# A decode kernel that streams its K and V caches: four batches interleaved over the partitions in 16 KB runs instead of two in 8 KB runs, with a permuted transpose and a new path to P^T

## The chip, the cores and the metric

The kernel runs on one core of one Trainium2 chip. The metric is the device time of one execution in microseconds (us). Before the change the median was 224.2 us in the first three runs (223.59 to 224.71). A run counts as slow when it is over 1.5% above the fastest of the same kernel.

Words used below. SBUF is the on-chip memory of 128 *partitions*; PSUM is the accumulator memory that TensorE writes. SP is the engine that issues nearly all of this kernel's DMA transfers, in program order. A *slot* is one buffer of a ring: a transfer into it may only be issued when the last user of its old content is done. The *granted clock* is the share of full speed that the throttle gave TensorE.

## The reference, cut to what matters

```python
# B=4 batches, one token each, D=576; 32 query heads on 16 K/V heads of 128; last 2048 cached tokens; F=4608
xn = layernorm(x)
q  = (xn @ wq)                                    # wq: 576 x 4096
s  = q . k_cache[:, :, -2048:, :] * 128**-0.5     # 4 x 32 x 2048 scores
p  = softmax(s)
o  = p . v_cache[:, :, -2048:, :]
a  = o @ wo                                       # wo: 4096 x 576
h  = gelu(layernorm(xn) @ w1)                     # then shifted, @ w2, added to xn -> x1
h2 = gelu(layernorm(x1) @ w3) @ w4                # w3: 576 x 4608, w4: 4608 x 576
out = x + a + x1 + h2
```

K and V are 33.5 MB each; the weights bring the bytes that must be read to 88.5 MB. At the 420 GB/s that the profile shows below this is 211 us: the kernel is a stream of reads with some arithmetic that has to fit beside it.

## The kernel before: the parts that matter

K and V are read in 32 units of 1 MB each. A unit is one K/V head of two of the four batches: partition p = 2i + b holds 32 consecutive tokens of batch b, so each partition receives a run of 8 KB.

```python
NKU = 7            # K slots of 1 MB
NVU = 9            # V slots of 1 MB
...
def kv_pairs(ring_t, slot, cache, u):
    g, pr = u // 2, u % 2
    return [(ring_t[:, slot * UE:(slot + 1) * UE],
             cache[pr:B:2, g, Sk - W:Sk, :].rearrange("b (i t) d -> i b (t d)", t=NT))]     # NT = 32
for u in range(NU):                              # NU = 32: all of K first
    ev_k.append(add_dma(kv_pairs(kring_t, u % NKU, A_k_cache, u), ("k", u % NKU),
                        [f"T{4 * (u - NKU) + 3}"] if u >= NKU else [], u))
wo_wait = f"T{4 * last_unit(NKU, 0, (_o - 1) // UE) + 3}"      # wo, w1, w2 reuse the K slots
for u in range(NU):                              # then V0..V8, wo, V9, V10, w1, w2, V11...
    w = [f"PV{u - NVU}"] if u >= NVU else (["q"] if u < WQ_SLOTS else [])
    ev_v.append(add_dma(kv_pairs(vring_t, u % NVU, A_v_cache, u), ("v", u % NVU), w, kk))
    if u == WO_AFTER - 1:                        # WO_AFTER = 9
        ev_wo = add_dma(..., "wo", [wo_wait], kk + 0.005)
...                                              # w3, and w4 in pieces of 12, 12, 8, 3 and 1 row tiles
```

K arrives with tokens on the partitions. TensorE transposes each 128x128 block of it with the identity, DVE and ACT copy the results from PSUM, and the scores are matmuls over the transposed K. After the last score comes the softmax. P is needed transposed too, and each batch of a unit needs zeros where the other batch's tokens lie:

```python
ins = e.transpose(tb[n % NTB][:, t, :], kring[:, u % NKU, 8 * k + t, :], ident_bf[:])       # T<n>
...
for q in range(4):                     # exp of 64 rows at a time, written interleaved into a zeroed P_sb
    for bh in range(2):
        s = slice(64 * bh, 64 * bh + 64)
        e.activation(out=P_sb[s, 8 * q:8 * q + 8, :, bh], in_=Sps[s, q, :]..., func=ACTF.Exp, ...)
...                                    # P^T: 32 transposes 128x128, four copies of 128x1024 out of PSUM
```

The probabilities times V are matmuls `PV<u>`; V slot u is free when `PV<u>` is done. A `T<n>` is a group of eight transposes; a K slot is free when the last group of its unit is done.

## Time and profile before

| | before |
|---|---|
| median of the first call | 224.45 us (four runs, 223.59 to 224.72) |
| span of the profiled execution | 223.1 us |
| DMA | 9 tenths or more in slices 2 to 38 of 40 |
| last byte of K landed (slowest of 16 DMA engines) | 96.7 us |
| last score done | 107.1 us |
| P^T ready | 118.8 us |
| last byte of w4 landed | 218.0 us |
| last output matmul done | 220.9 us |

The landing times come from the trace's semaphore updates: a transfer is split over 16 DMA engines, and "the first" and "the slowest" engine below stand for the first and the last of its 16 landings. Packet times and sizes come from the trace's packet records.

The first thing to look at is the table of 40 equal slices of the span (5.6 us each). Rows are TensorE's busy tenths, its granted clock in tenths, the busy tenths of the DMA engines, and the GB/s moved:

```profile
PE   0459999999999999997267722665993435997596
PEclk9999999999999999999755555555587555665579
DMA  6999999999999999999999999999999999999950
GB/s 249 426 420 422 420 422 419 420 422 416 419 422 417 417 422 420 420 420 417 422 414 413 412 412 419 422 417 419 420 420 417 422 416 426 419 414 410 409 210 1
```

DMA has no dip from slice 2 to slice 38, although TensorE is nearly full for the first half. Whatever the compute engines do, the queue always has a transfer that may start. The chain of waits, followed back from the end (start, duration, what), looks different at first sight; it runs through TensorE until 107 us, then through the softmax, then through DMA:

```profile
107.09 2.30 DVE rmax L357
...
117.81 1.03 ACT PT L379
118.98 1.01 PE ps L402 x32
120.00 13.21 DMA vring<-in_A_v_cache_dram
...
179.78 29.80 DMA vring<-in_B_w_dram
209.62 11.28 PE ps L423 x72
```

It names what released each step, not what the time is bound by. In the stretch before 118.98 us DMA never waits for TensorE: seven K slots, nine V slots and wo hold the work it does meanwhile. The kernel is bound by bytes until the first pieces of w4 are there, and by 72 output matmuls at the end. The transposes (L321) are the costliest group of TensorE, and the exponentials (L363) of the softmax; columns are busy time, mean ns of one, and the idle time before them with what ended it:

```profile
L321 PE MATMUL ps<-ident_bf,kring 128*128 128x128 bf16 x1024 | 66.7, 220 | 0.6 <-ACT regB L327 0.5
L363 ACT ACTIVATE P_sb<-ps,negb 64x512 bf16<-64x512 f32 x8 | 6.6, 824 | 2.6 <-DVE negb L358 2.5
```

The 0.6 us of idle time before 1,024 transposes says that TensorE, not DMA, paces the K stage: 5.39 us per head in the chain, while DMA needs about 4.95 us for its 2 MB.

### The profile page before, as it was taken

The numbers are of one execution on the slowest core, as the hardware profiler recorded it, in microseconds if no ns is written. First come the engines' busy times: TensorE is split into PE (matmuls) and PEld (weight loads), VectorE is DVE, ScalarE is ACT, GpSimd is POOL, SyncE is SP. The second block draws the span as 40 slices with busy tenths as digits, with TensorE's granted clock in tenths as the row PEclk, the third lists the DMA queues.
The fourth block names the chain that finished last, engine by engine and source line by source line (L and its number), as shares of the span: only waits on it lengthen the run. The fifth ranks groups of instructions, "written<-read, shape, count | busy, mean of one in ns | idle before, by whom it ended". The sixth has DMA issues, their size and how long they took to land.

```text
span 223.1 us, 6242 instructions
## 1 busy us (share of the span) xinstructions
PE 163.6 (73%) x2933; PEld 124.6 (56%) x2934; DVE 70.3 (32%) x124; ACT 62.1 (28%) x76; POOL 7.8 (4%) x14
## 2 busy tenths in 40 slices
PE   0459999999999999997267722665993435997596
PEld 0456777777777777775047722454573434576363
DVE  4803556666666556664441000051000000000000
ACT  2002555555555555555594000000200000000000
POOL 8500000000000000000000000000000000000000
PEclk9999999999999999999755555555587555665579
DMA  6999999999999999999999999999999999999950
GB/s 249 426 420 422 420 422 419 420 422 416 419 422 417 417 422 420 420 420 417 422 414 413 412 412 419 422 417 419 420 420 417 422 416 426 419 414 410 409 210 1
DMA packets 13682, 88.91 MB, mean 399 GB/s; under 512 B 1356, under 2 KB 1752, under 8 KB 4440
## 3 DMA queue, kind: packets, MB, share of 16 engines
q1 hardware_dynamic: 13640, 88.50, 96.1%
q8 instruction: 23, 0.38, 0.7%
q10 hardware_dynamic: 16, 0.01, 0.0%
q14 instruction: 3, 0.02, 0.0%
HBM read 88.49 MB, written 0.00 MB: 397 GB/s over the span
## 4 chain that ended last, share of the span: by engine, by line
DMA 43%; PE 40%; ACT 12%; issue 1%; DVE 1%; SPq 1%
DMA vring<-in_A_v_cache_dram 25%; PE ps L321 23%; DMA vring<-in_B_w_dram 13%; ACT regB L327 8%; PE ps L337 8%; PE ps L423 6%; DMA vring<-in_A_wq_dram 5%; ACT P_sb L363 3%; PE ps L402 2%; PE ps L309 1%; DVE rmax L357 1%; SPq L159 1%; PE ps L372 0%; ACT PT L379 0%; PE ps L294 0%
## 5 line engine op out<-in xcount | busy, mean ns | idle before, releaser
L321 PE MATMUL ps<-ident_bf,kring 128*128 128x128 bf16 x1024 | 66.7, 220 | 0.6 <-ACT regB L327 0.5
L321 PEld LDWEIGHTS ps<-ident_bf,kring 128*128 128x128 bf16 x1024 | 57.9, 98 | 14.1 <-issue 7.8
L328 DVE COPY regB<-ps 128x1024 bf16<-128x1024 bf16 x80 | 52.3, 687 | 36.0 <-PE ps L321 34.3
L327 ACT ACTIVATE regB<-ps 128x1024 bf16<-128x1024 bf16 x48 | 47.5, 1021 | 48.2 <-PE ps L321 48.2
L402 PE MATMUL ps<-PT,vring 128*128 128x4 bf16 x1024 | 30.6, 166 | 29.5 <-DMA vring<-in_A_v_cache_dram 26.7
L402 PEld LDWEIGHTS ps<-PT,vring 128*128 128x128 bf16 x1024 | 28.9, 103 | 33.6 <-DMA vring<-in_A_v_cache_dram 28.5
L337 PE MATMUL ps<-regB,Qpad 128*32 128x512 bf16 x256 | 17.6, 392 | 4.5 <-ACT regB L327 4.5
L513 ACT ACTIVATE h2T_sb<-ps 128x144 bf16<-128x144 f32 x1 | 0.3, 290 | 49.7 <-PE ps L507 49.7
L423 PE MATMUL ps<-kring,ORT 128*4 128x288 bf16 x64 | 13.7, 398 | 0.3 <-DVE ORT L441 0.3
L423 PE MATMUL ps<-vring,h2T_sb 128*4 128x288 bf16 x72 | 11.3, 328 | 2.6 <-DMA vring<-in_B_w_dram 2.6
L437 DVE TENSOR_TENSOR OTn<-ps,rinvB 128x64 bf16<-128x64 f32 (+2 forms) x3 | 0.6, 202 | 39.6 <-PE ps L402 39.6
L337 PEld LDWEIGHTS ps<-regB,Qpad 128*32 128x32 bf16 x256 | 5.3, 94 | 11.1 <-ACT regB L327 5.9
L423 PEld LDWEIGHTS ps<-vring,h2T_sb 128*4 128x4 bf16 x72 | 6.8, 96 | 6.8 <-DMA vring<-in_B_w_dram 2.7
L259 ACT ACTIVATE sd<-mv 4x1 f32<-4x1 f32 x3 | 0.6, 202 | 35.3 <-DVE mv L257 35.3
L423 PEld LDWEIGHTS ps<-kring,ORT 128*4 128x4 bf16 x64 | 7.0, 113 | 5.9 <-DVE ORT L441 0.4
L372 PE MATMUL ps<-ident_bf,P_sb 128*128 128x128 bf16 x32 | 4.1, 309 | 6.6 <-ACT P_sb L363 6.6
L475 DVE TENSOR_TENSOR x_bf<-ps,xn_bf 4x288 bf16<-4x288 f32 x2 | 0.9, 446 | 23.8 <-PE ps L470 23.8
L528 DVE CAST out_sb<-ps 4x288 bf16<-4x288 f32 x1 | 0.4, 446 | 24.0 <-PE ps L423 24.0
L372 PEld LDWEIGHTS ps<-ident_bf,P_sb 128*128 128x128 bf16 x32 | 3.1, 140 | 7.9 <-ACT P_sb L363 7.9
L363 ACT ACTIVATE P_sb<-ps,negb 64x512 bf16<-64x512 f32 x8 | 6.6, 824 | 2.6 <-DVE negb L358 2.5
L273 PE MATMUL ps<-ident_bf,xn_bf 4*128 4x4 bf16 x8 | 0.5, 166 | 8.8 <-DVE ragsrc L266 8.4
L498 PE MATMUL ps<-x1nT,regB 128*128 128x4 bf16 x144 | 5.2, 172 | 1.5 <-DMA regB<-in_B_w_dram 1.5
(78 smaller groups left out, 68.6 us busy)
## 6 DMA issues: line engine op xcount, KB each, us to landing
kring<-in_A_k_cache_dram SPq DMA_DIRECT2D x32, 1024.0 KB, 12.6
vring<-in_A_v_cache_dram SPq DMA_DIRECT2D x32, 1024.0 KB, 21.6
kring<-in_A_wo_dram SPq DMA_DIRECT2D x1, 4608.0 KB, 26.0
regB<-in_B_w_dram SPq DMA_DIRECT2D x4, 1152.0 KB, 27.0
vring<-in_A_wq_dram SPq DMA_DIRECT2D x4, 1024.0 KB, 7.9
vring<-in_B_w_dram SPq DMA_DIRECT2D x2, 1728.0 KB, 30.7
kring<-in_B_w_dram SPq DMA_DIRECT2D x2, 576.0 KB, 13.5
vring<-in_B_w_dram SPq DMA_DIRECT2D x1, 1152.0 KB, 30.2
```

The source lines that it names most:

```text
L159: e.dma_start(o_, i_).then_inc(S[skey], 16)
L309: ins = e.matmul(ps[:, 4 + (w % NTB), :], lhsT=zeros_bf[:, 0:128], rhs=zeros_bf[:, :], start=True, stop=True)
L321: ins = e.transpose(tb[n % NTB][:, t, :], kring[:, u % NKU, 8 * k + t, :], ident_bf[:])
L327: return "act", lambda e: e.activation(out=ktbuf[:, n % NKT], in_=tb[n % NTB], func=ACTF.Copy)
L328: return "dve", lambda e: e.tensor_copy(out=ktbuf[:, n % NKT], in_=tb[n % NTB])
L337: ins = e.matmul(Sps[32 * b:32 * b + 32, c4, :].rearrange("p (t i) -> p t i", t=8), lhsT=Qpad[:, g, b, :], rhs=ktbuf[:, n % NKT, :, bh:128:2],
L357: add("dve", lambda e: e.tensor_reduce(out=rmax[:], in_=Sps, axis=AX.XY, op=ALU.max), waits=[f"SC{G - 1}"], sig="rmax", key=KS)
L363: add("act", lambda e, q=q, s=s, bh=bh: e.activation(out=P_sb[s, 8 * q:8 * q + 8, :, bh], in_=Sps[s, q, :].rearrange("p (t i) -> p t i", t ...
L372: ins = e.transpose(PTps[q][:, t, :], P_sb[:, 8 * q + t, :, :].rearrange("p i b -> p (i b)"), ident_bf[:])
L402: ins = e.matmul(o_, lhsT=vring[:, u % NVU, t, :], rhs=r_, start=(t == 0), stop=(t == NT - 1))
L423: return e.matmul(ACC[h], lhsT=lhsT, rhs=rhs, start=start, stop=stop)
L498: ins = e.matmul(H2Tps[:, n, :], lhsT=w3main[:, r, lo:hi:st], rhs=x1nT[:, r, :], start=(r == 0 and n == 0), stop=False, skip_group_check=True)
```

## The change

The intent is longer runs for DMA and less work for ACT. A unit is now a K/V head of all four batches, 2 MB: partition p = 4i + b holds 64 consecutive tokens of batch b, a run of 16 KB. Transposing K with a permutation matrix instead of the identity sorts the columns by batch, so that scores read contiguous columns and the exponentials can take 128 rows at once. P^T is then made by 32x32 transposes on DVE and, for each of the four batches, a matmul with a quarter of a second permutation matrix, which moves that batch's rows to partitions 4i + b and leaves zeros elsewhere.

Units twice as large mean fewer slots: 3 for K and 4 for V, where there were 7 and 9 half as large. The four early V units are issued between the last K units, and wo, which reuses K slots, waits for the last transpose of K. The diff, cut to its core:

```diff
-NKU = 7
-NVU = 9
+NKU = 3
+NVU = 4
+V_EARLY = 4
...
-    NT = 32
+    NT = 64
...
+        def kv_src(cache, g):
+            return cache[:, g, Sk - W:Sk, :].rearrange("b (i t) d -> i b (t d)", t=NT)
+        def issue_k(g, key):
+            w = [f"T{8 * (g - NKU) + 7}"] if g >= NKU else []
...
+        for g in range(G):
+            issue_k(g, g)
+        for g in range(V_EARLY):
+            issue_v(g, G - V_EARLY + g - 0.5)      # ... K11 V0 K12 V1 K13 V2 K14 V3 K15
+        wo_wait = f"T{8 * (G - 1) + 7}"            # the last transpose of the last K unit
+        ev_wo = add_dma(..., "wo", [wo_wait], KS)
...                                                 # w1, w2, then V4.. as PV0.. free their slots
-        W4P = [(0, 3, 0), (3, 6, 2), (6, 8, 4)]
+        for c in range(8):                         # w4 in eight pieces (and two small ones)
...
-                    ins = e.transpose(tb[n % NTB][:, t, :], kring[:, u % NKU, 8 * k + t, :], ident_bf[:])
+                    ins = e.transpose(tb[n % NTB][:, t, :], kring[:, g % NKU, 8 * k + t, :], perm_bf[:])
...
+            add("act", lambda e, q=q, cs=cs: e.activation(out=P_sb[:, cs], in_=Sps[:, q, :], func=ACTF.Exp, ...
+            add("dve", lambda e, cs=cs: e.transpose(PTc[:, cs], P_sb[:, cs]), waits=[f"exp{q}"], ...
+        for m in range(16):
+            add("pe", ... e.matmul(PTps[m % 4], lhsT=permT[32 * b:32 * b + 32, :],
+                                   rhs=PTc[32 * b:32 * b + 32, 512 * q:512 * q + 512], start=True, stop=True), ...
...                                                 # 16 copies of 128x512 out of PSUM, 9 on DVE, 7 on ACT
```

Two smaller things come with it: wq and w3 are each read in two large transfers instead of four.

## The prediction

> **What bounds the kernel now.** The DMA engines. The table of 40 slices shows DMA at 9 tenths or more from slice 2 to 37, 409-426 GB/s. In the trace's packet records an 8192-byte packet takes 312 ns, 4608 bytes 181 ns, 9216 bytes 351 ns; the slowest of the 16 engines lands the last of w4 at 218.0 us, the first at 212.8. The chain of waits runs through TensorE until 107 us, but DMA never pauses there: while TensorE finishes K (5.39 us per head in the chain) and the softmax runs (107.1 to 118.8 us), the queue still holds V units and wo. The tail is TensorE's: 72 output matmuls, 209.6 to 220.9 us, start when the first 1.7 MB of w4 lands and end 2.9 us after the last landing; the clock is 0.5 for their first 4.7 us.
>
> **What the change does.**
> 1. 16 KB runs. From 312 and 351 ns I estimate 618 ns per 16 KB packet instead of 624: about 290 such packets per engine, -1.8 us.
> 2. w4 in eight pieces instead of three: the matmuls can start at about 10 us before the last landing instead of 8.4, and end about 0.9 us after it instead of 2.9: -2.0 us.
> 3. Half as many exponentials (128 rows instead of 64; 0.82 us and a 0.18 us accumulator read each): about -3.5 us of ACT. But four DVE transposes and 16 evacuations of 128x512 f32 (estimate 0.6 us each, from 2.29 us for 2048 f32 and 1.02 us for ACT's 1024) replace four evacuations; they take some 8 us after the first exponential. Softmax from the last score to P^T ready: about 13 us, against 11.8 now.
> 4. Transposes and scores: as before, 5.39 us per head.
> 5. The order of transfers. Before, K is read first, and nine V units follow while TensorE catches up. Now four 2 MB V units go before the last K unit, and wo waits for the last K transpose. The Trainium skill ("DMA: Bandwidth & Descriptors", Anatomy of one DMA) says a semaphore wait sits on the issuing sequencer, not in the DMA engines; so SP stops there, with nothing queued behind K15, and DMA stands idle while TensorE transposes the last unit: 5.4 us warm. But TensorE will have idled 3-5 us between the last K units, which arrive every 9.9 us; "TensorE: Matmul & The Clock Gate" (Part 1) has the clock halve after an idle window of about 3.4 us, and here it fell 1.5 us after the scores ended. I take 7.5 us, plus about 1.5 us from issue to first byte: +9.0 us.
> 6. wo, w1, w2 (about 15 us) then cover the softmax and the first PV product (2 us): together about 16 us after the last transpose. V4 waits for that PV: +1 us (0 to 4).
> 7. Three K slots against 5.39 us per head and 4.94 us of DMA per unit: around units 7-11 DMA starts to wait for slots: +0.5 us.
>
> **On the critical path:** 1, 2, 5, 6, 7. Sum: 224.2 - 1.8 - 2.0 + 9.0 + 1.0 + 0.5 = 230.9; I say 230.5 us, 226.5 to 234.5. Faster 3%, within 2% 25%, slower 72%.
>
> **What would show it.** DMA well below 9 tenths in slices near 115-125 us; SP waiting on the last K transposes there; a clock of 0.5 in it; 16 KB packets at 610-625 ns; the last output matmul within 1.5 us of the last landing; DVE and ACT both busy after the exponentials.
>
> **What would make it wrong.** 16 KB packets much faster than 618 ns; TensorE warm at the last unit (-2 us); slower P^T work; the slowest engine's lag (5 us by the end now) dissolving in the pause.

## The result, and the profile after

| | before | after |
|---|---|---|
| median (range), 4 runs each | 224.45 (223.59 to 224.72) | 236.16 (233.37 to 236.61) |
| ratio after/before, 95% interval | | 1.050 (1.042 to 1.059) |
| span of the profiled execution | 223.1 | 234.9 |

A ratio is the mean time of one kernel's fast runs over the mean of the other's in the same rounds, so it is not quite the ratio of the medians quoted beside it. The result of the changed kernel is correct. It is 11.7 us slower; the forecast was 230.5 us (6.3 us slower) with a range up to 234.5. Direction and cause of the largest part were right, the size was not.

The same four rows of the slice table (5.9 us per slice):

```profile
PE   0367999999999958396293479477498334994996
PEclk9999999999999999769978555555559555575569
DMA  7999999999999999999606997999999999999970
GB/s 258 421 433 435 413 399 385 419 373 407 410 393 399 419 430 424 427 435 426 276 0 224 418 390 307 416 427 438 413 430 438 413 433 424 428 433 393 410 314 10
```

Three things are new. First, a hole around slice 21, where DMA falls to 0 GB/s, with a second shallow dip at slice 25. Second, the rate *rises* above what it was before in some slices (433 to 438) and *falls* below it in slices 5 to 13 (373 to 419). Third, TensorE has gaps in slices 15 to 20, and its clock drops in two of them.

The hole, in stretches of 3 us (stretch, length, then busy time of PE, PEld, DVE, ACT and POOL with the number of instructions, granted clock, DMA share, GB/s):

```profile
111.00:114.00 3.00, 1.82 (x26) 1.32 (x24) 1.81 (x3) 2.05 (x2) 0.00 (x0) 1.00 1.01 431
114.00:117.00 3.00, 0.00 (x0) 0.00 (x0) 0.00 (x0) 0.00 (x0) 0.00 (x0) 1.00 0.46 191
117.00:120.00 3.00, 2.64 (x28) 1.91 (x32) 0.69 (x1) 0.79 (x1) 0.00 (x0) 0.58 0.00 0
120.00:123.00 3.00, 3.00 (x46) 1.95 (x38) 1.29 (x3) 0.75 (x2) 0.00 (x0) 0.85 0.00 0
123.00:126.00 3.00, 1.79 (x28) 1.22 (x32) 1.28 (x2) 2.27 (x3) 0.00 (x0) 1.00 0.26 31
```

Before, the stretch from 117 to 120 us had DMA at 1.01 and 405 GB/s. Read the table from top to bottom. At 114 us every compute engine is done with what it has and waits for the last K unit. K15 lands at 117.3 us, and at 117.5 us the clock falls to 0.5, the price of the wait, until 120.9 us (in `after_hot` below TensorE was kept busy through this wait, and the clock stayed at 1.0). Now TensorE works and DMA has nothing to do. The timeline says why; its lines are start, duration, engine and instruction, and in brackets the idle time before it:

```profile
93.14 0.53 SPq L161 DMA_DIRECT2D kring<-in_A_k_cache_dram  x1
117.36 1.81 PE L330 MATMUL ps<-perm_bf,kring 128*128 128x128 bf16 x16 [4.54 <-DMA kring<-in_A_k_cache_dram]
120.93 3.25 PE L330 MATMUL ps<-perm_bf,kring 128*128 128x128 bf16 x48
124.21 0.40 SPq L161 DMA_DIRECT2D kring<-in_A_wo_dram  x1
...
141.11 6.27 SPq L161 DMA_DIRECT2D vring<-in_A_v_cache_dram  x4
```

K15 was issued at 93.14 us. The next transfer in SP's order is wo, and it stands at a semaphore wait until the last transpose, at 124.21 us. Nothing can be issued past it. The Trainium skill ("DMA: Bandwidth & Descriptors", section "Anatomy of one DMA") says that a semaphore wait "happens on the issuing sequencer before dispatch", and that the DMA engines just consume their queues; this trace agrees: the engines emptied their queue at 116.88 us, moved nothing for 8.39 us, and the first packet of wo came at 125.27 us, 1.06 us after its issue. The second dip is V4, which waits for the first product with V (issued 141.11 us): 1.53 us without a packet.

The softmax did what was forecast, 12.6 us from the last score to P^T (forecast 13, before 11.8), and its parts have these sizes:

```profile
L370 ACT ACTIVATE regB<-ps,negb 128x512 bf16<-128x512 f32 x4 | 2.7, 686 | 2.5 <-DVE negb L366 2.5
L373 DVE STREAM_TRANSPOSE regB<-regB 128x512 bf16<-128x512 bf16 x4 | 2.8, 704 | 0.8 <-ACT regB L370 0.8
L386 DVE CAST PT<-ps 128x512 bf16<-128x512 f32 x9 | 5.7, 675 | 0.7 <-PE ps L378 0.7
L384 ACT ACTIVATE PT<-ps 128x512 bf16<-128x512 f32 x7 | 4.0, 596 | 3.3 <-PE ps L378 3.3
```

Exponentials take 2.7 us of ACT instead of 6.6; the 16 smaller copies (675 and 596 ns, estimated at 0.6 us) take the gain back. In the K stage the transposes (L330) show a new wait:

```profile
L330 PE MATMUL ps<-perm_bf,kring 128*128 128x128 bf16 x1024 | 71.5, 229 | 14.9 <-DMA kring<-in_A_k_cache_dram 14.6
```

TensorE now waited 14.6 us for K data; before, 0.6 us in all. Of it 13.4 us are four waits, of 1.8 to 4.7 us, for K12 to K15, in front of which the early V units are read; this is not the cost of the K slots. And the chain of waits at the end of the kernel:

```profile
187.36 28.98 DMA regB<-in_B_w_dram
216.39 2.51 PE ps L499 x72
220.84 11.85 PE ps L424 x72
```

Before, the output matmuls were released by a piece of w4; now they start when the product with w3 is done, which the last piece of w3 releases, and run 11.85 us without waiting for w4 at all.

A ledger of the 11.8 us between the two profiled executions, by the landing times of the slowest DMA engine:

| stretch | after minus before | what the terms of the prediction gave for it |
|---|---|---|
| until K15 has landed (in before: V7, at the same number of bytes) | +0.5 | -0.6: slots +0.5, 176 packets per engine at 6 ns each -1.1 |
| from there until all of V has landed | +10.6 | +9.4: pauses +9.0 and +1.0, 96 packets -0.6 |
| w3 and w4 | +1.5 | 0 |
| from the last landing to the end | -0.7 | -2.0 |
| sum | +11.8 | +6.8 (6.7 in its own sum, rounded down to +6.3) |

So there is no single miss: each of the four rows is 1.1 to 1.5 us worse than forecast. What stands behind the rows had to be tried.

### The profile page after: what moved, and what is told of

The parts are those of the page before. It is cut to its first block, busy times and chain, and to the rows that moved or that the text cites. A ratio compares the mean times of both kernels' runs of the same rounds, so it can differ in the third digit from the quotient of the medians.

```text
span 234.9 us, 6181 instructions
## 1 busy us (share of the span) xinstructions
PE 169.7 (72%) x2917; PEld 126.3 (54%) x2918; DVE 74.3 (32%) x134; ACT 61.4 (26%) x74; POOL 6.1 (3%) x20
## 4 chain that ended last, share of the span: by engine, by line
DMA 51%; PE 37%; ACT 6%; DVE 3%; SPq 1%; issue 1%
DMA kring<-in_A_k_cache_dram 24%; PE ps L330 19%; DMA vring<-in_A_v_cache_dram 15%; DMA regB<-in_B_w_dram 12%; PE ps L346 6%; PE ps L424 5%; PE ps L403 5%; ACT regB L336 4%; ACT PT L384 1%; DVE PT L386 1%; PE ps L499 1%; SPq L161 1%; DVE rmax L365 1%; DVE regB L373 1%; PE ps L378 1%
## 5 line engine op out<-in xcount | busy, mean ns | idle before, releaser
L330 PE MATMUL ps<-perm_bf,kring 128*128 128x128 bf16 x1024 | 71.5, 229 | 14.9 <-DMA kring<-in_A_k_cache_dram 14.6
L330 PEld LDWEIGHTS ps<-perm_bf,kring 128*128 128x128 bf16 x1024 | 62.1, 103 | 29.4 <-DMA kring<-in_A_k_cache_dram 16.2
L403 PE MATMUL ps<-PT,vring 128*128 128x8 bf16 x1024 | 29.2, 168 | 21.5 <-DMA vring<-in_A_v_cache_dram 20.3
L403 PEld LDWEIGHTS ps<-PT,vring 128*128 128x128 bf16 x1024 | 28.2, 103 | 24.8 <-DMA vring<-in_A_v_cache_dram 22.0
L346 PE MATMUL ps<-regB,Qpad 128*32 128x512 bf16 x256 | 18.4, 412 | 3.6 <-ACT regB L336 3.6
L424 PE MATMUL ps<-kring,ORT 128*4 128x288 bf16 x64 | 13.4, 393 | 0.3 <-DVE ORT L442 0.3
L424 PE MATMUL ps<-vring,h2T_sb 128*4 128x288 bf16 x72 | 11.8, 339 | 0.5 <-ACT h2T_sb L514 0.5
L378 PE MATMUL ps<-regB,permT 32*128 32x512 bf16 x16 | 5.9, 600 | 5.7 <-DVE regB L373 4.1
L303 PE MATMUL ps<-xnT,vring 128*128 128x4 bf16 x160 | 4.6, 166 | 5.4 <-DMA vring<-in_A_wq_dram 5.4
L499 PE MATMUL ps<-x1nT,regB 128*128 128x4 bf16 x144 | 5.0, 172 | 3.3 <-DMA regB<-in_B_w_dram 3.3
L303 PEld LDWEIGHTS ps<-xnT,vring 128*128 128x128 bf16 x160 | 4.4, 104 | 5.5 <-DMA vring<-in_A_wq_dram 5.5
L499 PEld LDWEIGHTS ps<-x1nT,regB 128*128 128x128 bf16 x144 | 4.9, 117 | 3.9 <-DMA regB<-in_B_w_dram 3.4
L378 PEld LDWEIGHTS ps<-regB,permT 32*128 32x128 bf16 x16 | 1.1, 99 | 10.5 <-DVE PT L386 5.3
```

Source lines behind the costliest of these rows:

```text
L303: ins = e.matmul(QTps[:, B * h:B * (h + 1)], lhsT=w, rhs=x_, start=(r == 0 and h == 0), stop=(r == 4), skip_group_check=True)
L330: ins = e.transpose(tb[n % NTB][:, t, :], kring[:, g % NKU, 8 * k + t, :], perm_bf[:])
L346: ins = e.matmul(Sps[32 * b:32 * b + 32, c4, :].rearrange("p (t i) -> p t i", t=16), lhsT=Qpad[:, g, b, :], rhs=kt[:, :, b, :], start=(g = ...
L378: add("pe", lambda e, m=m, q=q, b=b: e.matmul(PTps[m % 4], lhsT=permT[32 * b:32 * b + 32, :], rhs=PTc[32 * b:32 * b + 32, 512 * q:512 * q ...
L403: ins = e.matmul(OTps(g)[:, 8 * g:8 * g + 8].rearrange("p (b e) -> p b e", e=2), lhsT=vring[:, g % NVU, t, :], rhs=r_, start=(t == 0), sto ...
L424: return e.matmul(ACC[h], lhsT=lhsT, rhs=rhs, start=start, stop=stop)
```

## The experiments

The theory: the loss is in the order and in the slots, that is in stops of the DMA queue, and not in the new reads or the new arithmetic. Rival 1: the new path to P^T makes the loss. Rival 2: reading four batches in 16 KB runs is slower. All runs below gave correct results. Unless an edit says otherwise it is against the changed kernel. "Before" times quoted are those of the same call.

### Putting the early V units after the last K unit

```diff
-            issue_v(g, G - V_EARLY + g - 0.5)
+            issue_v(g, G - 1 + 0.1 * (g + 1))      # ... K14 K15 V0 V1 V2 V3, wo
```

> The changed kernel with one line different: the four early V units are issued after K15 instead of between the last K units. Order theory (the DMA queue runs dry while TensorE transposes K15, because wo waits for that and nothing is queued behind K15): the pause of about 8 us before wo and the 1.8 us before V4 go, DMA waits for K slots cost about 2 us more (K12 to K15 now also arrive at TensorE's 5.34 us a head): 227 us, 225.5 to 229. Rival 1 (the new P^T work, 16 evacuations, is what costs): still a pause before V4, at least 232. Rival 2 (16 KB packets over four batches are slower from HBM): no more than the pause is won, K still at 380-410 GB/s, and V and w3 slow as well.

Measured: 225.75 us (225.15 to 227.12), 1.006 (1.002 to 1.011) of before, which had 224.73. Most of the loss, some 10 us of it, is gone by moving four transfers by a few places, while all of the new arithmetic and all of the 16 KB runs stay. That settles rival 1, and most of rival 2. Its slices:

```profile
DMA  6999999999998999999999999999999999999970
GB/s 241 428 436 428 433 401 381 410 381 347 384 387 363 407 407 425 430 423 430 428 416 408 410 427 430 425 422 425 425 422 433 428 425 422 425 421 407 409 317 24
```

There is no hole any more; but slices 6 to 13 still run at 347 to 410 GB/s, so a second cost, independent of the order, is left in the K stage.

### Putting only V0 early

If the order behind K15 is the cause, it could also be mended by keeping three V units between the K units and moving one forward, or by combining both moves.

```diff
+            issue_v(g, 3.5 if g == 0 else G - V_EARLY + g - 0.5)       # v0_early
+            issue_v(g, 3.5 if g == 0 else G - 1 + 0.1 * g)             # both
```

> The changed kernel with V0 alone moved, from before K12 to after K3; V1 to V3 stay between the last K units, wo still waits for the last K transpose. Order theory: the dips of DMA in the first 75 us are waits for one of three K slots; V0 gives 4.9 us of slack, which TensorE's 0.45 us a head uses up only at the end, so the first 80 us run at 420 GB/s or more and about 3 us are won: 233 us, 231.5 to 234.5, with the pause of 8 us before wo still there. Rival 2 (the four-batch layout is slower from HBM): K stays at 380-410 GB/s and the time within 1 us of the changed kernel's 236.

> The changed kernel with V0 after K3 and V1 to V3 after K15: both repairs. Order theory: no pause anywhere, DMA at 9 tenths from slice 2 to the end; then the packets (611 ns for 16 KB against 624 for two of 8 KB, some 290 per engine) are worth about 3.5 us and the finer w4 about 0.5: 220.5 us, 219 to 222.5, faster than the kernel before. Rivals 1 and 2: still slower than the kernel before, 226 or more.

Measured: 238.27 us for the first (fast runs 1.057, 1.049 to 1.065, of before), so no better than the change itself; 227.58 us for the second, three of whose four runs were slow and also its profile, so that no ratio is given. Its one fast run, 223.94 us, is below the four of `v_last` (225.15 to 227.12), but one run does not settle which is faster. Both missed what was expected of them. The trace of `v0_early` shows a stop that can explain it:

```profile
45.19 1.51 PE L330 MATMUL ps<-perm_bf,kring 128*128 128x128 bf16 x16 [2.56 <-DMA kring<-in_A_k_cache_dram]
```

V0 in between K3 and K4 let TensorE run dry for 2.56 us while it was already catching up with three slots; its clock was 0.5 from 45.6 to 49.1 us. In a stage that TensorE paces, a stop of TensorE moves everything behind it. In the second kernel the same stop was 3.54 us (in its slow profile). The hole behind K15 stayed in the first one, as its order there is that of the change. I had thought of the V unit as work for DMA while a slot comes free; at that place it was work in front of the unit that TensorE needed.

### The same order in the kernel before

This is the reverse test: two-batch units of 8 KB runs, seven and nine slots, old softmax, and only the nine early V units moved in between the last nine K units.

```diff
-            kk = KS + 0.01 * u
+            kk = KS + 0.01 * u if u >= NVU else NU - NVU + u - 0.5
```

with wo, w1 and w2 kept behind K31.

> The kernel before with the order alone of the changed one: V0 to V8 (1 MB each) issued between the last K units, then wo, w1 and w2 waiting for the last K transpose, then V9. Everything else as before, 8 KB runs and old P^T. Order theory: DMA runs dry after K31 for the transposes of its 1 MB (2.6 us warm, about 4 cold) plus 1.1 us to the first byte and 1 us of slow restart, and again shortly before V9: 229.5 us, 227.5 to 232. Rivals 1 and 2 (P^T work, packet size): no difference to the kernel before, 224.5.

Measured: 231.36 us, 1.031 (1.026 to 1.035). The order alone costs the kernel before 6.9 us by this ratio. Its slices show the hole at the same place:

```profile
DMA  6999999999999999999926999999999999999970
GB/s 247 430 419 426 414 427 413 423 411 427 414 423 417 424 413 426 419 419 421 419 123 222 419 403 378 423 423 416 421 417 420 419 419 419 427 418 408 410 284 6
```

K31 landed at 118.90 us, wo was issued at 121.33 us, and DMA was without a packet for 3.92 us. That the hole is shorter than in the changed kernel fits the unit: behind a 1 MB unit half as many transposes remain. The rest of the 6.9 us is not accounted for here one by one.

### Four K slots and three V slots

The dips of the K stage remain in `v_last`. If they come from K slots, a fourth one should remove them; SBUF holds seven units, so one V slot has to go.

```diff
-NKU = 3
-NVU = 4
-V_EARLY = 4
+NKU = 4
+NVU = 3
+V_EARLY = 3
```

together with the order of `v_last`.

> The changed kernel with the early V units after K15 and four K slots and three V slots of 2 MB instead of three and four. Ring theory: what v_last still loses are DMA waits for K slots (K15 landed on the first engine at 97.4 us, unhindered it would be 92.2); moving V0 forward could not mend it because it starved TensorE, which needs 5.34 us a head against 4.89 us of DMA. A fourth slot lets DMA run ahead: K15 lands by about 93 us on the first engine, no slice of the K stage under 415 GB/s, 221.5 us (220 to 223.5), faster than v_last by 3 to 5 us. Rival (dips come from the four-batch 16 KB reads of K while TensorE and the evacuations use the memory): dips stay, time 225 or more.

Measured: 222.92 us (221.65 to 223.91), 0.993 (0.990 to 0.997) of before (224.25). The slices in which K lands (2 to 18) are now at 409 GB/s and over, with the very reads that rival 2 blames:

```profile
GB/s 238 427 427 427 430 427 433 430 427 423 427 421 421 430 418 409 424 423 427 354 420 407 294 427 427 427 424 433 427 424 368 427 427 427 424 423 405 412 390 35
```

Rival 2 falls. What three slots do can be read in the packet records. TensorE takes 5.34 us per head and DMA 4.89 us per unit, so DMA gains on TensorE until all slots are full, and from there on it waits for a slot at each unit. With three slots that is so from the start: K3 was issued at 26.72 us, when TensorE was done with K0, only 1.9 us before the first engine landed K2. In the kernel before, with seven slots of half the size, unit K7 was issued 9.9 us before K6 landed there, and K31 still 6.8 us before K30. In the changed kernel the nine units from K3 to K11 took 47.7 us on the first DMA engine, 5.30 us each, which is TensorE's pace, against 44.1 us at 4.89 us each: 3.6 us lost. A little over 1 us of it is time without a packet, in the mean of the engines; the larger part is that packets behind a wait are slow: of 1,468 16 KB packets between 20 and 80 us, 132 took over 1.15 times the median, against 8 of 1,550 with four slots (in a later run, below). Three small dips are left in this kernel (354, 294 and 368 GB/s): the wait of wo, that of V3 for the first product with V, and one from having only three V slots.

### 8 KB runs with everything else as in `k4v3`

How much do the 16 KB runs give? Each unit is read in two transfers of column halves, so that a partition gets two runs of 8 KB.

```diff
-... kv_src(A_k_cache, g))]
+... kv_src(A_k_cache, g)[:, :, h * UE // 2:(h + 1) * UE // 2]) for h in range(2)]
```

> k4v3 with every K and V unit loaded by two transfers of 8 KB runs (first and second half of the columns) instead of one of 16 KB runs; same bytes, same layout in SBUF. By packet times (611 against 2 x 312 ns, 256 packets per engine): 3.3 us slower than k4v3, if DMA is what bounds it throughout; if the 16 KB runs are worth nothing, within 1 us.

Measured: 224.36 us (0.999, 0.995 to 1.003, of before), 1.4 us more than `k4v3`, though the ranges overlap (222.57 to 225.36). By the packet records an 8 KB packet takes 312 ns and one of 16 KB 611 ns, so two small ones cost 13 ns more than one large one; with the 256 of K and V per engine 3.3 us would be lost. The trace shows where the rest went: K15 landed at 96.5 us instead of 95.4 and w2 at 126.3 instead of 124.8, by then 1.5 us late; but then V3 had to wait for the first product with V anyway, and landed at 131.4 us, even before the 132.2 us of `k4v3`. So in this run a gain in the rate of the reads was not kept across a wait for compute. The prediction had put 618 ns on such a packet, so the true gain per packet was twice the forecast, and still less arrived.

### w3 in four pieces, and w4 in eight in the kernel before

```diff
-                 for r in range(2)]                      # k4v3_w3x4: w3 in two transfers of 2F columns
+                 for r in range(4)]                      #            in four of F columns
```

> k4v3 with w3 in four transfers of 9 KB runs, as in the kernel before, instead of two of 18 KB. The tail theory: in the changed kernel the matmuls of two w3 quarters wait for the second transfer, so the output matmuls start 1.2 us later than w4's first piece allows; with four transfers they start 1.2 us earlier and the last matmul ends up to 1 us earlier, against 0.4 us of longer packets: 0.5 us faster than k4v3 (0 to 1.2).

Measured: 222.91 us, against 222.92 for `k4v3`: no difference. Smaller first pieces of w3 do not help, as its *last* piece releases the rest.

```diff
-        W4P = [(0, 3, 0), (3, 6, 2), (6, 8, 4)]
+        W4P = [(c, c + 1, c // 3 * 2) for c in range(8)]
...
-        W4N = [(12 * n, 12 * n + 12) for n in range(2)] + [(24, 32), (32, 35), (35, 36)]
+        W4N = [(4 * n, 4 * n + 4) for n in range(8)] + [(32, 35), (35, 36)]
```

> The kernel before with w4 alone loaded in eight pieces instead of three, and the output matmuls cut to match. Prediction on record: 2.0 us gained, 222.5. What the changed kernel's trace suggests instead (72 matmuls took 11.85 us there, at the clock of 0.5 for the first 5.9 us, and started only 1.3 us earlier before the last landing): about 1 us gained, 223.3 to 224.

Measured: 222.61 us (222.57 to 222.78), 0.993 (0.991 to 0.995): this one part of the change, alone on the kernel before, gives 1.6 us of the 2.0 forecast. The output matmuls in its timeline start without a wait for w4, and only the last 16 wait 0.26 us for its last pieces:

```profile
207.17 9.02 PE L423 MATMUL ps<-vring,h2T_sb 128*4 128x288 bf16 x56 [0.47 <-ACT h2T_sb L513]
216.45 2.22 PE L423 MATMUL ps<-vring,h2T_sb 128*4 128x288 bf16 x16 [0.26 <-DMA vring<-in_B_w_dram]
```

The last byte landed at 217.84 us and the last matmul ended 0.83 us later. In the changed kernel the same part gave only 0.7 us: the matmuls began 9.7 us before the last landing, took 11.85 us and ended 2.15 us after it. With `k4v3` and `k4v3_w3x4` (0.992 to 0.993 of before) it is among the three fastest kernels, which do not differ beyond their noise. It is 0.7% faster than before. `k4v3` has the eight pieces of w4 too, so all the rest of the change, 16 KB runs included, brings nothing net that these runs can see, even in the good order.

### A warm clock at the start, and a warm clock in the hole

The change's first head ran on a cold TensorE: the clock reached 1.0 at 25.3 us, in the kernel before at 19.8 us. More dummy matmuls at the start would mend that.

```diff
-N_WARM = 6
+N_WARM = 12
```

> The changed kernel with 12 warm-up matmuls instead of 6. In its trace the warm-ups end at 19.3 us, K0 lands at 20.4 and the clock rises only at 25.3, so the first head takes 7.2 us instead of 5.34, and by the wait for K slots that delays the following K units. If that is part of the loss: up to 1.9 us faster, 234.5 (233 to 236), and less spread between runs (the changed kernel's went from 233.4 to 236.6). If it is not: within 0.5 us of 236.2.

Measured: 237.45 us (234.76 to 238.35, one of six runs slow), the fast runs 1.055 (1.050 to 1.059) of before; its profile fell in the slow run. The clock was up at 20.2 us, but no time was won: the changed kernel without any edit took 237.41 us in a later call. In other executions of other kernels it was up at 19.5 us without help. The Trainium skill ("TensorE: Matmul & The Clock Gate", Part 1) calls the window that decides this free-running and the warm-up variable from run to run; the profiles here, from 19.0 to 25.5 us, agree that it varies.

For the hole, 20 matmuls of zeros keep TensorE busy between the transposes of K14 and K15.

```diff
+            for w in range(20):
+                ins = e.matmul(ps[:, 7, :], lhsT=zeros_bf[:, 0:128], rhs=zeros_bf[:, :], start=True, stop=True)
+        add("pe", pe_hot, waits=["xn2T"], sig="hot", key=8 * (G - 1) - 0.5)
```

> The changed kernel with 20 dummy matmuls of 128x512 zeros, into a PSUM bank that is free then, put between the transposes of K14 and K15, where TensorE waits 4.5 us. Theory of the pause: its length is the transposes of K15, 6.85 us in the trace because the clock was at 0.5 until 120.9 us, where a warm head has 5.3; with the dummies 1.5 us faster than the changed kernel, 234.7 (233.5 to 235.7), the clock at 1.0 through the pause. If the pause has another cause (DMA latency, the slow start of the rings): no difference.

The mechanism came out as expected. The transposes of K15 took 5.26 us, up to the issue of wo, instead of 6.85:

```profile
112.99 4.26 PE L363 MATMUL ps<-zeros_bf 128*128 128x512 bf16 x19
119.01 1.07 PE L330 MATMUL ps<-perm_bf,kring 128*128 128x128 bf16 x16 [1.75 <-DMA kring<-in_A_k_cache_dram]
120.98 3.25 PE L330 MATMUL ps<-perm_bf,kring 128*128 128x128 bf16 x48
124.27 0.39 SPq L161 DMA_DIRECT2D kring<-in_A_wo_dram  x1
```

16 transposes in 1.07 us here, in 1.81 us above. But wo was issued at the same time as before the edit, as K15 landed 1.65 us later. In the packet records a 16 KB packet of instructions was fetched from 116.83 to 117.93 us, and the last of the 16 completion packets of K15 came at 117.92 us, 1.04 us later than in the changed kernel; the data counts as landed only when all 16 have reported. The other 0.6 us lie between that packet and the landing and are not explained. The Trainium skill ("DMA: Bandwidth & Descriptors", "Queues, rings and completion order") says that the semaphore increment lands only after every earlier write of that engine, across its queues. The records agree, but an engine that was simply busy with the other packet would look the same, and they do not name the engine. The time is inconclusive: three of seven runs were fast, at 232.45 to 234.05 us (1.042 of before), four slow at 236.5 us and over; the change itself varies from 233.4 to 238.8 us over its two calls, and the profile fell in a slow run.

### Removing the remaining waits of `k4v3`

```diff
-        wo_wait = f"T{8 * (G - 1) + 7}"
+        wo_wait = f"T{8 * (G - 2) + 7}"        # k4v3_wo119: with four slots wo does not touch K15's
```

> k4v3 with wo waiting for the transposes of K14 instead of K15 (with four K slots wo, w1 and w2 lie in slots 0 to 2, K15 in slot 3). The short pause of DMA near 108 us goes. But V3 still waits for the first PV product, at the end of TensorE's K stage and the softmax, which DMA does not hold up any more: the pause near 124 us grows by as much. So no gain: 222.9, within 0.5 us of k4v3. If instead each pause of DMA cost its own length: 1 to 2 us faster.

Measured: 223.04 us (0.994 of before), the same as `k4v3`. The dip of wo's wait shrank, and the next grew:

```profile
GB/s 237 428 426 434 437 423 426 431 420 418 428 423 428 426 405 408 420 436 426 393 414 411 240 431 431 423 420 428 426 426 352 408 431 423 437 426 402 408 386 41
```

354 has become 393 and 294 has become 240: as expected, time saved in front of a wait is handed to the wait. To fill that one too, the first half of w3 was loaded before V3:

```diff
-... ("w3", r), ["PTt15"], KT + r)
+... ("w3", r), [f"SC{G - 1}"] if r == 0 else ["PTt15"], KT + r if r else KS + 0.3)      # before V3
-        ev_w3.append(add_dma([(w3rag, rag_src(B_w3))], ("w3", 4), [], KT + 4))
+        ev_w3.append(add_dma([(w3rag, rag_src(B_w3))], ("w3", 4), [], KS + 0.4))
```

> k4v3_wo119 with the first half of w3 (2.4 MB, waits for the last scores instead of the last P^T product) and its ragged part (0.6 MB, free space) loaded after w2, ahead of V3, instead of after V15. This puts 7 us of transfers where DMA waits for the first PV product. If that wait is what is left: DMA at 9 tenths from 3 to 160 us, 2.5 to 4 us faster than k4v3_wo119: 219.8 (218.5 to 221), faster than both kernels.

Measured: 224.93 us, 1.004 (1.001 to 1.007) of before, slower than `k4v3`, although its last byte landed at 215.32 us, 2.5 us earlier than in `k4v3`, and the row of DMA in its slices has no dip left:

```profile
DMA  6999999999999999999999999999999999999920
```

Its timeline at the end:

```profile
202.53 4.86 PE L499 MATMUL ps<-x1nT,regB 128*128 128x4 bf16 x144
209.33 11.64 PE L424 MATMUL ps<-vring,h2T_sb 128*4 128x288 bf16 x72 [0.47 <-ACT h2T_sb L514]
```

TensorE's tail now bound the end: it does the product with w3 (L499) only after all of V, and then the output matmuls, at a clock of 0.5 until 214.8 us. One more kernel moved three of the five passes over w3 in front of the last V products:

```diff
+... key=KT + r if r in (2, 3) else KV + 25.5 + 0.01 * r        # h2_0, h2_1, h2_4 before PV13
```

> k4v3_w3early with the matmuls of the w3 parts that land early (first half and ragged part) placed before PV13 instead of after the last product with wo. If TensorE's work after the last V unit is what made k4v3_w3early slow (224.9): 2.5 to 4 us faster, 221.5 (220.5 to 222.5), and the output matmuls start by 206 us. If it is something else: within 1 us of 224.9.

Measured: 223.53 us, 0.999 (0.995 to 1.002) of before. Half of L499 was out of the way, but the output matmuls started at 207.51 us, later than the 206 expected at most, and took 11.77 us. So the reads could be made to end earlier than in any other kernel here, and the time did not follow: in these two kernels the end is bound by 72 matmuls, about half of their time at a clock of 0.5, rather than by bytes.

### Settling the slots: the change twice, with three and with four K slots

The slots had only been tested in the good order. The changed kernel unedited, and with `NKU = 4, NVU = 3, V_EARLY = 3` in its own interleaved order, ran in the same rounds.

> The changed kernel as it is, as the base of after_k4v3: 236 us, 233 to 237, in two groups near 233.5 and 236.5 if the spread comes from one DMA engine that is 1.6 us later when K15 lands in some executions (118.96 against 117.31 us in two traces).

> The changed kernel with four K slots and three V slots, and three V units instead of four between the last K units; the order otherwise as it was, wo waits for the last K transpose. Slot theory: no dips in the first 75 us, the K stage 2.8 us shorter; the pause before wo stays at about 8 us; one V unit less in between leaves the sum of DMA work as it is: 233.3 us (231.5 to 234.5), 2 to 3.5 faster than after_again. If K slots cost nothing on balance: within 1 us of it.

Measured: 237.41 us (1.061, 1.057 to 1.064) and 233.04 us (1.040, 1.036 to 1.044): 4.4 us for one slot more in K and one less in V (and three early V units instead of four). In the slices of the second one, the K stage lost its dips and the hole stayed:

```profile
GB/s 257 428 431 430 413 439 422 428 426 422 425 425 433 416 430 425 419 440 279 0 272 418 365 328 425 425 436 419 428 425 422 430 425 433 428 426 397 407 351 19
```

And its timeline around the hole:

```profile
110.02 1.07 PE L330 MATMUL ps<-perm_bf,kring 128*128 128x128 bf16 x16 [2.35 <-DMA kring<-in_A_k_cache_dram]
115.28 0.39 SPq L161 DMA_DIRECT2D kring<-in_A_wo_dram  x1
```

Here TensorE was warm when K15 came (1.07 us for 16 transposes, 5.26 us for the unit) and the hole was 6.79 us instead of 8.39. So of the 4.4 us, 1.6 is a shorter hole and 2.8 is left for the K stage. This 2.8 is a difference between medians and one pair of profiles, not a measurement; in the good order the same swap, from `v_last` to `k4v3`, also gave 2.8 us, between medians. Both are near the 3.6 us from the landing times, which do not count what the lost V slot costs.

## Why the prediction was right in direction and wrong in size

**What bounds the kernel before: right.** Bytes until w4, then output matmuls. `before_w4x8`, which only lets those start earlier, gained 1.6 us.

**Step 5, the pause behind K15: right.** Forecast 9.0 us, measured 8.39 us without a packet (6.85 us of transposes at a clock partly 0.5 instead of 7.5, 1.06 us from issue to first packet instead of the 1.5 taken, and 0.4 us between the last packet of K15 and its landing, which had no term). `v_last` removed it by the order alone, and `before_mixed` brought a pause into the other kernel by the order alone.

**Step 6, the second pause: right.** Forecast 1 us, measured 1.53.

**Steps 3 and 4, softmax and transposes: right.** 12.6 us against 13, and 5.34 us per head against 5.39. The softmax became a little longer although ACT's exponentials shrank by 3.9 us.

**Step 7 failed:** "Three K slots against 5.39 us per head and 4.94 us of DMA per unit: around units 7-11 DMA starts to wait for slots: +0.5 us." The two rates were right; the place and the size were not. DMA was held to TensorE's pace from K3 on, not from units 7 to 11, and it cost 3.6 us by the landing times and about 2.8 us by `after_k4v3`. The step credits DMA with a lead that lasts for some seven units. In fact three slots gave it a lead of only 1.9 us, each unit from K3 to K11 took TensorE's pace (5.34 against 4.89 us, nine units), and behind each wait came slow packets: a mean of 640 ns per 16 KB in that stretch against 617 ns with four slots.

**Step 1 was mis-sized, in its favour, and did not pay:** a 16 KB packet took 611 ns, not 618, which would be worth 3.8 us instead of 1.8. In the K stage TensorE sets the pace, so a faster read only fills the slots sooner; there the gain turned into the waits of step 7. `k4v3_8k` measured what the whole kernel keeps of it in the good order: 1.4 us.

**Step 2 was mis-sized:** -2.0 us forecast, -0.7 measured in the changed kernel. The sum had an error of its own: 11.28 us of matmuls that start 10 us before the last landing cannot end 0.9 us after it. They started 9.7 us before and took 11.85 us. Alone on the kernel before, the same edit gave 1.6 us.

**A term was missing:** the last stretch, w3 and w4, took 1.5 us longer on the slowest DMA engine, though the first engine took no longer than before (25.2 against 25.4 us). When all of V had landed the slowest engine was 1.9 us behind the first, and 3.5 us at the end. I had listed the lag only as something that might dissolve in the pause; it did become small there, and grew again.

**What stays open.** Of the 10.6 us of the middle stretch, 8.39 + 1.53 - 1.25 (96 packets at 13 ns) = 8.7 us are accounted for. The other 1.9 us are argued to be the slow restart of the queue behind each pause and the different times at which the 16 engines stop and start; no run separates the two. The packet records give the first a size: in the 5 us behind the two pauses the packets took, summed per engine, 1.1 us longer than their medians. In the first stretch, 3.6 us lost less 2.3 us for 176 packets at 13 ns would be 1.3 us; the slowest engine shows 0.5 and the first one 2.3, so that rest isn't settled either. Why the changed kernel spreads from 233 to 239 us while the kernel before stays within 1.8 us, and whether a warm TensorE in the hole saves time over many executions, is not known.

## What to carry to other kernels

When a kernel is bound by its stream of reads, ask for each transfer in the queue what its issue waits for and what is still queued in front of it: a transfer that waits for the *newest* data needs other transfers between that data and itself, and here moving four of them was worth about 10 us. Larger units mean fewer slots, and the gain of a longer run (1.4 us kept) is small beside a stage that loses its slack (about 3 us here). Cost a slot limit as the difference of the two paces times the number of units after the lead is used up, and check whether a time saved in front of a wait is only handed to that wait.

## What the Trainium skill lacked or had wrong

- "DMA: Bandwidth & Descriptors", "Bandwidth" gives rates by the size of a transfer (341 GB/s for 1 MB) and says that about 358 GB/s binds on the HBM side, beside its own 425 for 16 MB; a note there gives 358 as the share of a core when both cores of a pair stream. Here, on one core with the queue kept full, the kernel before moved 409 to 426 GB/s in transfers of 1 MB, and 397 GB/s over its whole span. The section has no figure for the length of a run within a transfer: 312 ns per 8 KB packet and 611 ns per 16 KB.
- No page that I found says that a queue that has run dry restarts slowly: 132 of 1,468 packets over 1.15 times the median with three K slots, 8 of 1,550 with four; and the first seven packets of V4, behind 1.53 us without a packet, took 1.00 to 1.21 us against a median of 0.61.
- The same page, "Latency and other measured facts", gives about 600 ns to the first byte of a transfer issued in hardware; behind a pause it was 1.06 us from the issue of wo to its first packet.
- "Runtime: NRT & Kernel Launch", "Instruction fetch mechanics", has instructions fetched by DMA in blocks of 16 KiB and calls the cost mostly hidden. It gives no time for a fetch beside a full data queue: 23 packets of 16 KB per execution, 1.0 to 1.1 us each in the kernel before (0.9 to 1.3 us in the changed one), and one of them came just before the late completion of a K unit in `after_hot`.
- "TensorE: Matmul & The Clock Gate", Part 1, has the clock rise after a busy window. In the kernel before, TensorE ran back to back from 118.98 to 126.3 us, all but two of its matmuls having 4 columns, and the clock stayed at 0.5; so here being busy by the profile for 7.4 us was not enough.
